# Switching the PE array to the 64-row mode and back once per four chunks instead of once per two, in a kernel that hides convolution work behind its matmuls

**The chip, the cores and the metric.** One core of one Trainium2 chip. The metric is the device time of one execution in microseconds (us), as a median. An execution of one core has no die partner to compare with, so the clock that TensorE was granted is given where it matters: the profiles record it. "PE" is TensorE; its weight loads are a separate stream beside its matmuls.

## The reference

One block of a transformer: a modulated LayerNorm, a long convolution with gates, a residual, a second modulated LayerNorm, and a SwiGLU feed-forward network. S = 2048 rows, D = 576 features, F = 4608 hidden features, all bfloat16. Cut to what matters:

```python
h = layernorm(x) * (1 + ca) + sa
kv = causal_4_tap(k, shift_k) * v
y = irfft(rfft(pad(kv)) * rfft(pad(ssm_k)))[:S] + kv * ssm_D     # the convolution
x = x + ga * (h * y)
h = layernorm(x) * (1 + cb) + sb
x = x + gb * ((silu(h @ w1) * (h @ w3)) @ w2)                    # the feed-forward network
```

The convolution is causal, so rows can be done block by block: the kernel works on four row blocks of 512 rows.

## The kernel before

After an opening, in which the first rows go through the convolution and a half-width first stage of products runs, the kernel has for each of four row blocks a *gate/up stage* (`stream`: `h @ w1` and `h @ w3`, evicted and multiplied) and a *down projection* (`down`: the product with `w2`). The convolution of the next row block is a Python generator of small steps. `advance(cost)` emits steps worth `cost` planned microseconds at that place of the program, so that they run beside the products. Most of the convolution is VectorE work (spectra multiplied and summed), but it also has TensorE matmuls (transposes, spectra at L313, inverse transforms at L539), ScalarE copies of their results, LayerNorm passes on ScalarE, and six tiny scalar computations for each LayerNorm on GpSimd.

A contraction over D = 576 is four full matmuls of 128 rows and 64 rows that are left. The 64-row matmuls of gate and up run two at a time, one in each half of the array, and that needs another row mode of the PE array.

```python
self.psum = pool("psum", bufs=4, ...)   # tiles of two banks: all of PSUM
self.hp = pool("hp", bufs=2)            # staging of sg and u

def full(k, first):     # 8 (or 16 narrow) matmuls over 128 rows, both products
    ...
def rest(k, first):     # the 64-row ones, gate in rows 0-63, up in rows 64-127
    ...
def hide(k):
    (fc, t0, t1, _, _), fi, m = items[k]
    sg = self.hp.tile([P, RB], BF16, name="sg", tag="sg")
    nc.scalar.activation(sg[:], gus[k][:, 0, :], ACT.Silu)              # L934, ScalarE
    u = self.hp.tile([P, RB], BF16, name="u", tag="u")
    nc.scalar.copy(u[:], gus[k][:, 1, :])                               # L936, ScalarE
    f = fc * FC + fi
    nc.vector.tensor_mul(self.h3[:, f:f + m, t0:t1], sg[:]..., u[:]...) # L938, VectorE
    del gus[k]
    self.advance(rate * 2.05)
# begin(k): weights, and gus[k] = a PSUM tile
for k in range(0, len(items), size):
    early, late = range(k, k + size // 2), range(k + size // 2, k + size)
    for m in early:
        begin(m)
        full(m, True)
    for m in early:
        rest(m, False)
    for m in late:
        begin(m)
        rest(m, True)
    for m in early:
        hide(m)
    for m in late:
        full(m, False)
        hide(m)
# ... cut ...
self.stream(r, jobs, rate, 4 if r == NRB - 1 else 2)
```

An item `k` is one PSUM tile of results. A group runs full, half, half, full, so that the mode changes twice per group. The scheduler keeps the order of each engine's instructions as they are emitted, more or less, and in the traces below each engine takes its instructions in that order. Line numbers are those of the kernel that ran: they shift by a line or a few between the kernels (`down` is L979 before and L980 after).

Of the kernel before, what the change touches and what calls it, by code (L numbers as in the profile page):

```python
# [24 lines left out]
NRB = S // RB  # L25
# [18 lines left out]
class _Kernel:  # L44
# [840 lines left out]
    def stream(self, r, jobs, rate, size):  # L885





        nc = self.nc
        hT = self.h2T[r % 2]
        items = []
        for job in jobs:
            m = RB // (job[2] - job[1])
            items += [(job, fi, m) for fi in range(0, FC, m)]
        gus, ws = {}, {}

        def load(job):
            fc, _, _, w, ahead = job  # L900
            if ahead is not None:
                ahead()
            if w is None:
                if fc not in self.w13:
                    self.load_w13(fc)
                w = self.kept[fc] = self.w13.pop(fc)
            ws[job[0:3]] = w


        def full(k, first):  # L910
            (fc, t0, t1, _, _), fi, m = items[k]
            w, n = ws[fc, t0, t1], t1 - t0
            for a in range(m):
                for i in range(2):
                    for ct in range(4):
                        nc.tensor.matmul(gus[k][:, i, a * n:(a + 1) * n],  # L916
                                         w[:, 5 * i + ct, (fi + a) * P:(fi + a + 1) * P], hT[:, ct, t0:t1],
                                         start=(first and ct == 0 and a == 0),
                                         stop=(not first and ct == 3 and a == m - 1))

        def rest(k, first):
            (fc, t0, t1, _, _), fi, m = items[k]
            w, n = ws[fc, t0, t1], t1 - t0
            for a in range(m):
                for i in range(2):
                    rows = slice(64 * i, 64 * i + 64)
                    nc.tensor.matmul(gus[k][:, i, a * n:(a + 1) * n],  # L927
                                     w[rows, 4, (fi + a) * P:(fi + a + 1) * P], hT[rows, 4, t0:t1],
                                     start=(first and a == 0), stop=(not first and a == m - 1))

        def hide(k):
            (fc, t0, t1, _, _), fi, m = items[k]
            sg = self.hp.tile([P, RB], BF16, name="sg", tag="sg")
            nc.scalar.activation(sg[:], gus[k][:, 0, :], ACT.Silu)  # L934
            u = self.hp.tile([P, RB], BF16, name="u", tag="u")
            nc.scalar.copy(u[:], gus[k][:, 1, :])  # L936
            f = fc * FC + fi
            nc.vector.tensor_mul(self.h3[:, f:f + m, t0:t1], sg[:].rearrange("p (a t) -> p a t", a=m),  # L938
                                 u[:].rearrange("p (a t) -> p a t", a=m))
            del gus[k]  # L940
            self.advance(rate * 2.05)

        def begin(k):
            if items[k][1] == 0:
                load(items[k][0])
            gus[k] = self.ps()
# [8 lines that stand above are left out]
                begin(m)  # L955
                rest(m, True)
            for m in early:
                hide(m)
            for m in late:
                full(m, False)  # L960
                hide(m)

    def down(self, r, rate):
        nc = self.nc
# [62 lines left out]
    def row_blocks(self, n1):  # L1027
        for r in range(NRB):
            cost = 0
            if r + 1 < NRB:  # L1030
                s0 = 2 * r + 2

                self.begin(self.conv(s0), FIRST_DUE if r == 0 else 0.0)
                cost = CONV_US[r]
            time = 110.0 * 0.85 - (N1 * 1.03 if r == 0 else 0)
            rate = cost / time
            if r == 0:

                jobs = [(fc, 256, 512, self.kept[fc], None) for fc in (n1 - 2, n1 - 1)]

                new = [(n1 + i, 0, RB, None, (lambda: self.keep_x(0)) if i == 1 else None)
                       for i in range(NF // FC - n1)]
                again = [(fc, 256, 512, None, None) for fc in range(n1 - 2)]
                while new or again:
                    jobs += new[0:1] + again[0:1]
                    new, again = new[1:], again[1:]
            else:
                jobs = [(fc, 0, RB, None, None) for fc in range(NF // FC)]
            self.stream(r, jobs, rate, 4 if r == NRB - 1 else 2)
            self.down(r, rate)  # L1050
            self.end()

# [52 lines left out]
```

## Time and profile before

521.53 us (521.48 to 521.57, three executions); the profiled execution spans 518.3 us.

| stage (from its first matmul to the next stage's) | us |
|---|---|
| opening, to the first transpose of the first row block | 68.9 |
| first block: gate/up, with the transposes ahead of it; down | 62.95; 39.54 |
| second block: gate/up; down | 78.22; 41.31 |
| third block: gate/up; down | 78.29; 38.01 |
| fourth block: gate/up; down (no convolution left) | 71.85; 35.48 |

The chain that ended last, followed back through whatever released each step:

```profile
PE 84%; DMA 8%; ACT 4%; DVE 2%; issue 1%; POOL 1%; DVEq 0%
```

Nearly all of the time is TensorE itself. The second is TensorE's timeline at the start of the first block's convolution. Columns: start, duration, engine, line, operation, output and inputs, count, and in brackets how long the engine was idle just before and what ended that.

```profile
78.81 0.41 PE L313 MATMUL ps<-kT,Fk 128*128 128x288 bf16 x2
79.94 1.91 PE L916 MATMUL ps<-h2T,wst 128*128 128x256 bf16 x16 [0.72 <-ACT W L315]
81.78 0.61 PE L927 MATMUL ps<-h2T,wst 64*128 64x256 bf16 x8
82.78 0.41 PE L313 MATMUL ps<-kv,Fb 128*128 128x288 bf16 x2 [0.39 <-ACT u L936]
```

Between one pair of spectrum matmuls (L313) and the next there is product work, 1.91 + 0.61 us of it here.

### The profile page before, as it was taken

To read this page: it belongs to the slowest core of one execution; us is meant where nothing else is said; L and a number is where in the kernel's file an instruction comes from. 1 tells how busy PE (TensorE), PEld (TensorE's weight loads), DVE (VectorE), ACT (ScalarE), POOL (GpSimd) and SP (SyncE) were. 2 spreads that over 40 slices of the span, in tenths; PEclk is the share of its full clock that TensorE was granted. 3 is DMA by queue.
4 is the path that set the end of the run, shared out by engine and by line. 5 is a ranking of instruction groups with operands and counts; after the bars stand their busy time and mean duration, and the time that the engine had idled before them with its cause. 6 is when DMAs were issued, how large, how long until landed. Compare 5 with 4: busy or idle time off the path is not lost.

```text
span 518.3 us, 8731 instructions
## 1 busy us (share of the span) xinstructions
PE 499.9 (96%) x3362; PEld 293.8 (57%) x3362; DVE 341.0 (66%) x515; ACT 293.3 (57%) x581; POOL 54.9 (11%) x109
## 2 busy tenths in 40 slices
PE   7999988999999999999998999999999999999997
PEld 3666765555788444444676543434588544444775
DVE  8898996999995355896999995389661212222012
ACT  6668469668543469759561465876816446445000
POOL 3205001204021001202002000120101000000000
PEclk9999889999999999999999999999999999999999
DMA  8959629757679953547999894554455453450462
GB/s 269 313 178 332 201 89 321 275 183 250 197 208 348 330 176 107 188 158 275 363 365 352 318 284 150 165 178 156 152 143 145 147 173 119 161 169 10 118 179 70
DMA packets 102205, 107.77 MB, mean 208 GB/s; under 512 B 5075, under 2 KB 94228, under 8 KB 102164
## 3 DMA queue, kind: packets, MB, share of 16 engines
q1 hardware_dynamic: 102142, 107.21, 64.3%
q8 instruction: 26, 0.43, 0.3%
q14 instruction: 15, 0.12, 0.1%
q10 hardware_dynamic: 22, 0.01, 0.0%
HBM read 96.00 MB, written 11.21 MB: 207 GB/s over the span
## 4 chain that ended last, share of the span: by engine, by line
PE 84%; DMA 8%; ACT 4%; DVE 2%; issue 1%; POOL 1%; DVEq 0%
PE ps L916 46%; PE ps L979 25%; PE ps L927 7%; DMA wst<-in_B_w_dram 5%; DMA w2t<-in_B_w_dram 3%; PE ps L313 2%; PE ps L539 2%; PE ps L364 1%; PE ps L299 1%; ACT junk L440 1%; PE ps L571 1%; PE ps L219 0%; PE ps L626 0%; ACT sg L934 0%; DMA shk_raw<-in_A_shift_k_dram 0%
## 5 line engine op out<-in xcount | busy, mean ns | idle before, releaser
L916 PE MATMUL ps<-h2T,wst 128*128 128x512 bf16 (+1 forms) x1344 | 267.4, 351 | 5.9 <-DMA wst<-in_B_w_dram 3.0
L916 PEld LDWEIGHTS <-wst 128*128 128x128 bf16 x1344 | 128.1, 98 | 128.6 <-issue 19.7
L934 ACT ACTIVATE sg<-ps 128x512 bf16<-128x512 f32 x144 | 86.6, 601 | 117.0 <-PE ps L927 73.9
L979 PE MATMUL ps<-w2t,h 128*128 128x288 bf16 x1152 | 145.6, 286 | 3.1 <-DMA w2t<-in_B_w_dram 2.3
L979 PEld LDWEIGHTS <-h 128*128 128x128 bf16 x1152 | 112.2, 98 | 32.5 <-issue 4.0
L938 DVE TENSOR_TENSOR h<-sg,u 128x512 bf16<-128x512 bf16 x144 | 60.5, 422 | 96.6 <-ACT u L936 96.6
L936 ACT CAST u<-ps 128x512 bf16<-128x512 f32 x144 | 84.5, 587 | 0.2 <-DVE h L938 0.2
L410 DVE TENSOR_TENSOR p<-X,V 128x3456 bf16<-128x3456 bf16 x28 | 54.7, 1953 | 5.1 <-DMA X<-Xd 4.9
L412 DVE TENSOR_TENSOR z<-z,p 128x3456 bf16<-128x3456 bf16 x28 | 54.7, 1954 | 0.2
L997 DVE TENSOR_TENSOR og<-ps,gbrow 128x288 bf16<-128x288 f32 x32 | 13.2, 450 | 48.9 <-PE ps L979 48.9
L927 PE MATMUL ps<-h2T,wst 64*128 64x512 bf16 (+1 forms) x336 | 43.2, 355 | 0.4 <-ACT kT L366 0.4
L440 ACT ACTIVATE junk<-x 128x576 bf16<-128x576 bf16 x54 | 37.5, 695 | 0.5
L601 ACT ACTIVATE h2T<-ps,sbcol,cbcol 128x256 bf16<-128x256 bf16 x35 | 16.7, 569 | 24.8 <-PE ps L571 24.8
L927 PEld LDWEIGHTS <-wst 64*128 64x128 bf16 x336 | 11.6, 95 | 28.1 <-issue 24.1
L455 POOL TENSOR_SCALAR l2m<-l2s 128x2 f32<-128x2 f32 x6 | 8.9, 1476 | 153.3 <-ACT junk L440 153.3
L334 DVE TENSOR_TENSOR kvt<-kh,shk 128x1152 bf16<-128x1152 bf16 x24 | 18.1, 753 | 7.4 <-DMA kh<-in_A_k_dram 7.2
L455 POOL TENSOR_SCALAR l1m<-l1s 128x2 f32<-128x2 f32 x7 | 6.5, 929 | 139.4 <-ACT junk L440 139.4
L566 ACT ACTIVATE h2row<-x,l2n,l2r 128x576 bf16<-128x576 bf16 (+1 forms) x24 | 13.7, 642 | 12.5 <-POOL l2n L460 12.4
L335 DVE TENSOR_TENSOR kv<-kv,kvt 128x1152 bf16<-128x1152 bf16 x24 | 18.1, 753 | 0.3
L315 ACT CAST X<-ps 128x576 bf16<-128x576 f32 x24 | 15.5, 658 | 0.0
L405 DVE TENSOR_TENSOR z<-X,V 128x3456 bf16<-128x3456 bf16 x7 | 13.7, 1953 | 2.5 <-DMA X<-Xd 2.5
L745 ACT CAST y<-ps 128x576 bf16<-128x576 f32 x14 | 8.4, 651 | 10.2 <-PE ps L539 10.2
(137 smaller groups left out, 356.3 us busy)
## 6 DMA issues: line engine op xcount, KB each, us to landing
wst<-in_B_w_dram SPq DMA_DIRECT2D x80, 512.0 KB, 4.5
w2t<-in_B_w_dram SPq DMA_DIRECT2D x72, 288.0 KB, 3.2
X<-Xd SPq DMA_DIRECT2D x8, 864.0 KB, 5.8
Xd<-X SPq DMA_DIRECT2D x6, 864.0 KB, 6.4
wst<-in_B_w_dram SPq DMA_DIRECT2D x80, 64.0 KB, 2.2
kh<-in_A_k_dram SPq DMA_DIRECT2D x7, 720.0 KB, 6.9
Vd<-V SPq DMA_DIRECT2D x4, 864.0 KB, 6.3
V<-Vd SPq DMA_DIRECT2D x4, 864.0 KB, 5.0
```

Source lines behind the costliest of these rows:

```text
L334: nc.vector.tensor_mul(tmp[:], kh[:, 3 - j:5 - j, :], tap(j))
L335: nc.vector.tensor_add(kv[:], kv[:], tmp[:])
L410: nc.vector.tensor_mul(p[:], X[:], V[:])
L412: nc.vector.tensor_add(z[:], z[:], p[:])
L440: self.nc.scalar.activation(junk[:], src[:, i, :], func, accum_out=out[:, col:col + 1])
L601: nc.scalar.activation(dst, src, ACT.Identity, bias=self.sbcol[:, ct:ct + 1], scale=self.cbcol[:, ct:ct + 1])
L916: nc.tensor.matmul(gus[k][:, i, a * n:(a + 1) * n], w[:, 5 * i + ct, (fi + a) * P:(fi + a + 1) * P], hT[:, ct, t0:t1], start=(first and ct ...
L927: nc.tensor.matmul(gus[k][:, i, a * n:(a + 1) * n], w[rows, 4, (fi + a) * P:(fi + a + 1) * P], hT[rows, 4, t0:t1], start=(first and a == 0 ...
L934: nc.scalar.activation(sg[:], gus[k][:, 0, :], ACT.Silu)
L936: nc.scalar.copy(u[:], gus[k][:, 1, :])
L938: nc.vector.tensor_mul(self.h3[:, f:f + m, t0:t1], sg[:].rearrange("p (a t) -> p a t", a=m), u[:].rearrange("p (a t) -> p a t", a=m))
L979: nc.tensor.matmul(acc[t], self.h3[:, f0 + f, t * P:(t + 1) * P], w[:, f, :], start=(f0 + f == 0), stop=(f0 + f == NF - 1))
```

## The change

The intent: groups of four in all 512-row stages, so that the mode changes half as often, as the fourth block already did. Because a group of four holds all four PSUM tiles, no convolution step is emitted behind its first two members, and a double portion behind each of the other two, so that a convolution matmul finds a tile that the first members have left. The opening stage keeps its pairs.

```diff
-        def hide(k):
+        def hide(k, go):
@@
-            self.advance(rate * 2.05)
+            if go:
+                self.advance(go * rate * 2.05)
@@
             for m in early:
-                hide(m)
+                hide(m, 1 if size == 2 else 0)
             for m in late:
                 full(m, False)
-                hide(m)
+                hide(m, 1 if size == 2 else 2)
@@
-            self.stream(r, jobs, rate, 4 if r == NRB - 1 else 2)
+            self.stream(r, jobs, rate, 4)
```

## The prediction

> **What bounds the kernel now.** I read the page first, then the chain of waits in two stretches, then busy time by stage, then the VectorE and DMA rows of the one stage where TensorE is not alone.
>
> ```profile
> PE 499.9 (96%) x3362; PEld 293.8 (57%) x3362; DVE 341.0 (66%) x515; ACT 293.3 (57%) x581; POOL 54.9 (11%) x109
> L916 PE MATMUL ps<-h2T,wst 128*128 128x512 bf16 (+1 forms) x1344 | 267.4, 351 | 5.9 <-DMA wst<-in_B_w_dram 3.0
> L927 PE MATMUL ps<-h2T,wst 64*128 64x512 bf16 (+1 forms) x336 | 43.2, 355 | 0.4 <-ACT kT L366 0.4
> ```
>
> TensorE is busy 96% of the span, and the two groups here are the gate/up products: L916 contracts over 128 rows, L927 over the 64 rows left of 576. Mean durations overlap, so I price a matmul by start-to-start distance, from the chain. Second row block (one feature chunk is 16 full matmuls and 4 half-row ones per two chunks), then the last row block, which already has groups of four:
>
> ```profile
> 212.71 0.54 PE ps L927 x4
> 213.25 3.56 PE ps L916 x16
> 216.81 0.54 PE ps L927 x4
> 217.34 3.56 PE ps L916 x16
> ```
>
> ```profile
> 418.86 0.97 PE ps L927 x8
> 419.83 7.01 PE ps L916 x32
> 426.84 0.97 PE ps L927 x8
> ```
>
> Two chunks repeat every 216.81 - 212.71 = 4.10 us, so four cost 8.19 (4.095 x 2 over several periods); a group of four repeats every 426.84 - 418.86 = 7.98. The difference, 0.21 us, is one pair of row-mode changes. It also comes out bottom up: 16 full matmuls with no change before them take 3.45 us (0.2158 each), with a change 3.56; four half-row matmuls run two at a time, 2 x 0.2158 = 0.43, and take 0.54. So each change costs about 0.105 us. Nothing else fills these stretches: the chain is TensorE end to end.
>
> Busy time by stage (first row block's products, second's, last's):
>
> ```profile
> core 0: us, PE busy (x) PEld busy (x) DVE busy (x) ACT busy (x) POOL busy (x), PEclk, DMA share, GB/s
> 72.00:132.60 60.60, 56.98 (x411) 34.48 (x411) 55.48 (x72) 46.22 (x95) 11.06 (x18) 0.97 0.68 228
> 171.60:250.00 78.40, 78.40 (x405) 32.64 (x404) 54.75 (x82) 57.90 (x117) 7.95 (x18) 1.00 0.62 207
> ```
>
> In the second row block TensorE is full and VectorE has slack. In the first, VectorE is busy 55.5 of 60.6 us, and TensorE waits a little, mostly for weights (0.5, 0.5 and 1.1 us at 86, 100 and 127.6).
>
> **What the Trainium skill says.** "TensorEngine Tiling (Array Packing)", Tiling Modes, Key Properties: "Changing tiling mode (not just tile) drains the TensorE". The trace agrees and gives the price, 0.105 us. "TensorE: Matmul & The Clock Gate", Back-to-back issue gap, puts isolated N=512 matmuls at about 216 ns when warm; here 215.8. "PSUM — Partial Sum Buffer", Specifications, gives 8 banks per partition of 512 FP32 values: the pool's four two-bank tiles are all of it, so a group of four holds the whole of PSUM until its first members are evicted. The trace of before cannot show that beside convolution work, since its only groups of four (last row block) have none.
>
> **The change part by part.** *Removed: mode changes.* An item is one fill of a PSUM tile: a chunk of 128 features by 512 rows, or two chunks by 256 rows. The first row block has 24 items after the unchanged opening stage (12 of single chunks, 12 of paired ones), the second and third 36 each. Groups of two make 12 + 18 + 18 = 48 pairs of changes, groups of four 6 + 9 + 9 = 24. Gain 24 x 0.211 = 5.06 us, all on TensorE, all on the path where TensorE is the bound. No matmul is added or dropped.
>
> *Moved: instruction order.* I compared the built orders. In the last group of the second row block the scheduler splits the half-row work: one half-row matmul, eight full, five half-row, two full, two half-row. That is three pairs of changes in place of one, and a half-row matmul alone in its slot: 2 x 0.211 + 0.216 = 0.64 us back.
>
> *Moved: convolution steps.* They now come in two double portions per group. One step unit is 1.037 x 2.05 in the second row block, so 4.25 us of planned work at once, and nothing behind the first two members. In the second and third row blocks I stepped through the groups by hand with before's durations (eviction 2 x 0.5 to 0.6, convolution copy 0.52, product and sum 1.9 each). Relative to the group's start the first two are evicted by about 4.9 and 6.1 us, the third begins full matmuls at 4.5 and ends at 6.3, so a convolution tile issued then finds a free buffer; the fourth ends at 8.0. The inverse transforms (L539) sit after the seventh and eighth group, and VectorE's last input for them is ready at least 0.3 us earlier. I charge no stall but 0.1 here and there: net gain 18 x 0.211 - 0.64 - 0.3 = 2.9 us.
>
> *First row block.* Gain 6 x 0.211 = 1.27, against three losses that I find:
> - First group: the transposes and six spectrum matmuls move behind the third and fourth member. ScalarE then has a chain of four statistics passes (0.68) alternating with four copies (0.52), an eviction and two 0.77 us rows just before the next group, so the next group starts near 85.9 instead of an effective 85.5, and VectorE's first spectrum sum slips from 83.3 to about 86.
> - Weights: two groups mix two weight chunks whose second loads only when the previous group is done (5.5 to 5.7 us in the chain), but its half-row products now come 4.0 us after that and need all four pieces. Before, 4 of its full matmuls could run first. About 0.8 and 0.4 us more wait.
> - The inverse transform there stands between the third and fourth member of the fourth group, and its second half needs a VectorE sum that I place at 111.9, some 1.5 us after TensorE gets there; from then on ScalarE's evictions wait for VectorE's products (two staging buffers only), and the last two groups lose another 1 to 2 us waiting for PSUM.
>
> Together about 4 us lost for 1.27 gained: the first block ends 2.7 us later. The down projection behind it is TensorE-bound and VectorE catches up in it, so the delay stays and does not grow. Sum: 521.5 + 2.7 - 2.9 = 521.3; as my by-hand waits are a pessimistic reading (any slack that I missed shortens them), I put 520.9.
>
> **The rivals.**
> 1. *Pure saving*: TensorE stays the only bound, the waits in the first block don't appear. For it: second and third block show no TensorE wait at all, and VectorE's order is nearly unchanged in item numbers. Against: VectorE is busy 92% in the first block and starts later. Time 521.5 - 5.06 + 0.64 = 517.1.
> 2. *PSUM starvation*: with all four tiles held, convolution tiles wait for evictions in every group, about 1 us in each of the 12 groups of the second and third block that have convolution matmuls. For it: four buffers, double portions. Against: the built order puts these matmuls where before's durations find free tiles. Time 521.3 + 12 = 533 at worst, 525 with a third of it.
> 3. *Weight loads become the bound*: 8.0 instead of 8.2 us per weight chunk; loads land in 4.5 us median and the last block runs at 7.98 with no weight wait, so only the mixed groups of the first block are exposed, as counted.
>
> **Range and chances.** Between rival 1 and a mild form of rival 2: 517.0 to 525.0 holds it 8 times in 10. Two per cent is 10.4 us. Faster by that would need double the whole of the removed cost; slower needs rival 2 in full. Hence 0.01 faster, 0.96 within, 0.03 slower.
>
> **What would show each step.** Right: in the second and third block the chain repeats every 7.98 us with 7.01 and 0.97 us pieces wherever there is no convolution matmul; one stretch near the end of the second block with a lone half-row matmul; TensorE's waits on weights in the first block growing to about 1.4 us each, a wait of L539 on VectorE there, and TensorE idle of 4 us or so more than now in that stage, whose end moves from 132 to about 135. Wrong: waits of L313 or L916 on ScalarE spread over all groups (rival 2), or a first block that ends at 131 or earlier (rival 1). A period other than 7.98 would void the price of a change itself.

## The result

**529.55 us** (527.43 to 530.08, four executions) against 521.55 us (521.48 to 522.79) on the same chip: ratio 1.014, 95% interval 1.0108 to 1.0172. A ratio here is the mean time of one kernel's fast executions over that of the other's in the same rounds, so it is not quite the ratio of the medians. Executions over 1.5% slower than the fastest of the same kernel are left out of the means. The changed kernel is 8 us slower, inside the 2% class and outside the predicted range of 517 to 525 us. The clock is not the reason: its executions were granted 0.990 to 0.997 of full speed, and its profiled execution took 527.43 us at 0.997 where that of the kernel before took 520.12 us at 0.992.

The profiled executions span 525.5 and 518.3 us. The stages, from the two traces:

| stage | before | after | difference |
|---|---|---|---|
| opening (unchanged code) | 68.94 | 67.63 | -1.31 |
| first block gate/up | 62.95 | 66.79 | +3.84 |
| first block down | 39.54 | 40.33 | +0.79 |
| second block gate/up | 78.22 | 79.84 | +1.62 |
| second block down | 41.31 | 41.56 | +0.25 |
| third block gate/up | 78.29 | 79.41 | +1.12 |
| third block down | 38.01 | 38.89 | +0.88 |
| fourth block, both | 107.33 | 107.32 | 0 |

They sum to +7.2 us, which is the difference of the spans. The page's lines that answer to those of before, and its chain:

```profile
PE 496.5 (94%) x3362; PEld 296.6 (56%) x3362; DVE 341.6 (65%) x515; ACT 292.2 (56%) x581; POOL 47.2 (9%) x109
...
PE 64%; DVE 16%; ACT 10%; DMA 7%; issue 3%; POOL 1%; SPq 0%; ACTq 0%
...
L916 PE MATMUL ps<-h2T,wst 128*128 128x512 bf16 (+1 forms) x1344 | 263.0, 349 | 6.5 <-DMA wst<-in_B_w_dram 1.8
...
L927 PE MATMUL ps<-h2T,wst 64*128 64x512 bf16 (+1 forms) x336 | 39.3, 348 | 1.1 <-ACT u L936 0.8
```

TensorE is busy for 3.4 us less (499.9 to 496.5), so part of the saving is there, but not all of the 3.4 us is saving: 1.5 us of it lies in the first block, where the clock differed. Before's profile has a stretch at half clock there, which that of the changed kernel has not (first block of each; then that stretch):

```profile
68.94:131.89 62.95, 58.09 (x424) 35.17 (x422) 57.76 (x76) 48.37 (x99) 11.06 (x18) 0.97 0.66 219
67.63:134.42 66.79, 56.59 (x425) 35.43 (x422) 57.31 (x76) 47.97 (x99) 9.66 (x18) 1.00 0.68 212
73.02:76.43 3.41, 3.41 (x27) 2.22 (x25) 3.34 (x3) 1.14 (x3) 0.00 (x0) 0.50 0.00 0
```

The columns are those of the prediction (start and end, length, busy us of PE, PEld, DVE, ACT and POOL, then granted clock, DMA share and GB/s). The same code at a clock of 1.00, in run 4's profile below, takes 61.97 us in the first block. So at like clocks the first block loses 4.8 us, and not 3.84. The other gate/up stages ran at 1.00 in every profile of this document, so their lengths compare directly; the first block's clock lies between 0.95 and 1.00.

The span grew, and the chain says who took over: TensorE's share fell from 84% to 64%, and VectorE's rose from 2% to 16% and ScalarE's from 4% to 10%. The saving itself is in the second block just as predicted:

```profile
221.76 0.97 PE ps L927 x8
222.73 7.01 PE ps L916 x32
229.74 0.97 PE ps L927 x8
```

Busy time of the second block's stage, with the same columns:

```profile
174.75:254.59 79.84, 77.57 (x405) 33.86 (x403) 53.70 (x82) 56.38 (x114) 5.90 (x18) 1.00 0.62 203
```

In the second block TensorE, which had no idle time at all before, is now idle for 79.84 - 77.57 = 2.27 us, in four waits: 0.74 and 0.27 us for a convolution copy (X, L315), and these two for an eviction copy:

```profile
235.92 0.41 PE L313 MATMUL ps<-kv,Fb 128*128 128x288 bf16 x2 [0.68 <-ACT u L936]
236.90 3.61 PE L916 MATMUL ps<-h2T,wst 128*128 128x512 bf16 x16 [0.57 <-ACT u L936]
```

The eviction of that group begins at 234.80 us, 0.1 us after a product of VectorE's (L938) that stood behind a step of 1.96 us. Three places in the other blocks show the same kinds of wait.

**First block, first group.** The same spectrum matmuls as above, now all behind the third and fourth member:

```profile
80.38 0.71 ACT L440 ACTIVATE junk<-x 128x576 bf16<-128x576 bf16 x1
...
81.06 0.65 ACT L315 CAST W<-ps 128x576 bf16<-128x576 f32 x1
...
81.76 0.41 PE L313 MATMUL ps<-kv,Fb 128*128 128x288 bf16 x2 [0.80 <-ACT W L315]
...
82.96 0.41 PE L313 MATMUL ps<-kv,Fb 128*128 128x288 bf16 x2 [0.80 <-ACT Wo L315]
...
84.16 1.02 PE L916 MATMUL ps<-h2T,wst 128*128 128x512 bf16 x4 [0.80 <-ACT Wo L315]
```

No product matmuls stand between the last of them any more. The three shown wait for the copy of an earlier spectrum, which gives back a PSUM tile; ScalarE makes these copies at its own pace of one LayerNorm pass and one copy, 1.2 us per 0.41 us of TensorE work. With a wait of 0.77 us at 79.36 us, for the copy of the transposed rows (kT, L366), that makes four waits, which replace the 0.72 and 0.39 us of before.

**First block, inverse transform.** TensorE stands still for VectorE's sums:

```profile
106.95 0.76 DVE L525 TENSOR_TENSOR z<-z 128x1152 bf16<-128x1152 bf16 x1
107.62 1.96 DVE L410 TENSOR_TENSOR p<-X,V 128x3456 bf16<-128x3456 bf16 x1
...
109.49 0.76 DVE L526 TENSOR_TENSOR z<-z 128x1152 bf16<-128x1152 bf16 x1
...
110.31 0.66 PE L539 MATMUL ps<-z,Fb 128*128 128x288 bf16 x4 [1.87 <-DVE z L526]
```

A step of 1.96 us from another part of the convolution stands between the two sums in VectorE's queue.

**Third block, first group.** This is the longest single wait of the two full stages, and it goes through three engines:

```profile
302.11 1.96 DVE L410 TENSOR_TENSOR p<-X,V 128x3456 bf16<-128x3456 bf16 x1
...
303.99 0.75 DVE L938 TENSOR_TENSOR h<-sg,u 128x512 bf16<-128x512 bf16 x2
304.50 0.60 ACT L934 ACTIVATE sg<-ps 128x512 bf16<-128x512 f32 x1 [2.31 <-DVE h L938]
...
304.99 0.58 ACT L936 CAST u<-ps 128x512 bf16<-128x512 f32 x1
305.46 1.14 ACT L366 COPY kT<-ps 128x1152 bf16<-128x1152 bf16 x1
...
306.65 0.65 PE L313 MATMUL ps<-kT,Fk 128*128 128x288 bf16 x4 [1.79 <-ACT kT L366]
```

VectorE is in a long step, so two products (L938) wait. The two staging buffers are full, so ScalarE's next eviction waits 2.31 us. The convolution's copy stands behind that eviction in ScalarE's queue, and TensorE waits 1.79 us for the copy. ScalarE's waits of this kind in the whole kernel (us in total, times, longest), before and after:

```profile
ACT sg L934 <- DVE h L938: 7.4, 6, 1.7
```

```profile
ACT sg L934 <- DVE h L938: 11.9, 10, 2.3
```

### The profile page after: what moved, and what is told of

The parts are those of the page before. It is cut to its first block, busy times and chain, and to the rows that moved or that the text cites. A ratio compares the mean times of both kernels' runs of the same rounds, so it can differ in the third digit from the quotient of the medians.

```text
span 525.5 us, 8723 instructions
## 1 busy us (share of the span) xinstructions
PE 496.5 (94%) x3362; PEld 296.6 (56%) x3362; DVE 341.6 (65%) x515; ACT 292.2 (56%) x581; POOL 47.2 (9%) x109
## 4 chain that ended last, share of the span: by engine, by line
PE 64%; DVE 16%; ACT 10%; DMA 7%; issue 3%; POOL 1%; SPq 0%; ACTq 0%
PE ps L916 35%; PE ps L980 17%; PE ps L927 5%; DVE p L410 5%; DVE z L412 3%; ACT junk L440 3%; DMA h<-in_w_mod_dram 2%; ACT sg L934 2%; ACT u L936 2%; DMA wst<-in_B_w_dram 2%; PE ps L539 1%; ACT hg L500 1%; DVE h L938 1%; DMA w2t<-in_B_w_dram 1%; DMA V<-Vd 1%
## 5 line engine op out<-in xcount | busy, mean ns | idle before, releaser
L916 PE MATMUL ps<-h2T,wst 128*128 128x512 bf16 (+1 forms) x1344 | 263.0, 349 | 6.5 <-DMA wst<-in_B_w_dram 1.8
L938 DVE TENSOR_TENSOR h<-sg,u 128x512 bf16<-128x512 bf16 x144 | 59.9, 423 | 103.3 <-ACT u L936 103.2
L927 PE MATMUL ps<-h2T,wst 64*128 64x512 bf16 (+1 forms) x336 | 39.3, 348 | 1.1 <-ACT u L936 0.8
L927 PEld LDWEIGHTS <-wst 64*128 64x128 bf16 x336 | 13.6, 94 | 25.1 <-issue 17.1
L455 POOL TENSOR_SCALAR l2m<-l2s 128x2 f32<-128x2 f32 x6 | 3.3, 556 | 155.2 <-ACT junk L440 155.2
L539 PE MATMUL ps<-z,Fb 128*128 128x288 bf16 x80 | 11.8, 287 | 4.9 <-DVE z L526 3.4
L455 POOL TENSOR_SCALAR l1m<-l1s 128x2 f32<-128x2 f32 x7 | 2.7, 382 | 152.4 <-ACT junk L440 152.4
L315 ACT CAST X<-ps 128x576 bf16<-128x576 f32 x24 | 15.3, 657 | 0.0
```

The lines of the kernel that those rows point to most:

```text
L539: nc.tensor.matmul(ps[:, h, 0:H], self.Fb[:, b, cs], z[:, row, h * H:(h + 1) * H], start=(i == 0), stop=(i == len(terms) - 1))
L916: nc.tensor.matmul(gus[k][:, i, a * n:(a + 1) * n], w[:, 5 * i + ct, (fi + a) * P:(fi + a + 1) * P], hT[:, ct, t0:t1], start=(first and ct ...
L927: nc.tensor.matmul(gus[k][:, i, a * n:(a + 1) * n], w[rows, 4, (fi + a) * P:(fi + a + 1) * P], hT[rows, 4, t0:t1], start=(first and a == 0 ...
L938: nc.vector.tensor_mul(self.h3[:, f:f + m, t0:t1], sg[:].rearrange("p (a t) -> p a t", a=m), u[:].rearrange("p (a t) -> p a t", a=m))
```

## The experiments

Four theories grew in this order. **A**: holding all four PSUM tiles turns any delay of an eviction into a stall. **B**: portions that are held back and doubled bunch the convolution and make VectorE late. **C**, from the second run: VectorE's unbroken runs starve GpSimd, and ScalarE stands behind GpSimd. **D**, after eleven runs: the two staging buffers carry VectorE's delay over to ScalarE and from there to TensorE. "First block" below is always counted from its transposes. All eighteen gave right results. "Before" is the kernel before, timed in the same rounds; its medians were 521.4 to 522.1 us. A stage length is from one profiled execution.

**1 and 2: each half of the change alone.** Groups of four with one portion behind every member:

```diff
-                hide(m, 1 if size == 2 else 0)   # early
+                hide(m, 1)
-                hide(m, 1 if size == 2 else 2)   # late
+                hide(m, 1)
```

> Groups of four in every full stage, but convolution steps behind every member in single portions, as before. Theory A (the loss comes from holding all four PSUM tiles while convolution work needs tiles too): as slow as the changed kernel or slower, 528 to 533 us, because convolution matmuls now stand right behind the half-row matmuls, when no tile is free until the first member is evicted. Rival B (the loss comes from doubling and delaying the convolution portions): near the pure saving, 516 to 519 us.

Measured: 528.85 us, ratio 1.0106 (1.0067 to 1.0146). The second block's stage takes 81.36 us, longer than in the changed kernel. This is theory A, in one line of the waits (us in total, times, longest):

```profile
PE ps L313 <- ACT u L936: 5.7, 10, 0.9
```

Ten times a spectrum matmul needs a PSUM tile, and every one is held by a member of the group that ScalarE is still evicting. The down projections of the first and third block stay at 39.74 and 38.12 us. That of the second has 45.26 us, with a wait of ScalarE for GpSimd of 12.7 us in it. The total is in theory A's range.

Pairs as before, but no portion behind the first and a double one behind the second member:

```diff
-                hide(m, 1 if size == 2 else 0)   # early, the three blocks
+                hide(m, 0)
-                hide(m, 1 if size == 2 else 2)   # late
+                hide(m, 2)
-            self.stream(r, jobs, rate, 4)
+            self.stream(r, jobs, rate, 4 if r == NRB - 1 else 2)
```

> Groups of two as before in the first three row blocks, but no steps behind the first member and a double portion behind the second. Theory A: two tiles stay free, so little is lost, 521 to 523.5 us. Rival B: loses what the changed kernel loses plus the saving that it does not have, 528 to 535 us.

Measured: 533.41 us, ratio 1.0222 (1.018 to 1.0264): slower than the whole change, with two PSUM tiles free. So neither half is innocent, and the halves do not add. The first block takes 70.39 us (at a clock of 0.96), and the largest part of that excess is one event:

```profile
122.31 9.30 POOL L455 TENSOR_SCALAR l2m<-l2s 128x2 f32<-128x2 f32 x1 [25.61 <-ACT junk L440]
...
133.42 2.29 ACT L566 ACTIVATE h2row<-x,l2n,l2r 128x576 bf16<-128x576 bf16 x4 [8.60 <-POOL l2n L460]
...
136.71 1.22 PE L364 MATMUL ps<-ident,knat 128*128 128x128 bf16 x10 [5.73 <-ACT u L936]
```

A GpSimd instruction on two numbers per partition lasts 9.30 us where its neighbours last 0.2 to 0.7. It ends at 131.61 us, 0.09 us after VectorE's run of back-to-back two-input instructions. ScalarE waits for it, the evictions behind that in its queue wait, PSUM stays full, and TensorE stands for 5.73 us.

**3 and 4: where, and the price.** The changed kernel with the first block back in pairs, and the kernel before with its fourth block in pairs too:

```diff
-            self.stream(r, jobs, rate, 4)
+            self.stream(r, jobs, rate, 4 if r else 2)      # run 3
-            self.stream(r, jobs, rate, 4 if r == NRB - 1 else 2)
+            self.stream(r, jobs, rate, 2)                  # run 4
```

> The changed kernel with groups of two and single portions in the first row block alone. If the losses of the blocks add up as its trace shows (3.8 us in the first block's products, 0.8 in the down projection behind it, 1.6 and 1.1 in the second and third block's products): 529.5 - 4.6 = about 525 us. If the later losses were only an echo of a late first block: 517 to 519 us.

> The kernel before with groups of two in the last row block, which has no convolution work beside it: nine more pairs of row-mode changes at 0.211 us. If the price read from the chain holds: 521.5 + 1.9 = 523.4 us. If a change is hidden or dearer in some other way: outside 522.9 to 523.9.

Measured: 522.64 us, ratio 1.0007 (0.9974 to 1.004), which is between the two expectations, and 523.3 us, ratio 1.002 (0.9996 to 1.0043). With the first block in pairs, that block takes 62.43 us and its down projection 39.46 us, as before. The second and third stage still take 79.85 and 79.56 us. The two kinds of reading do not quite agree here. By the stages from the transposes on, run 3 loses 4.4 us against the profile of before, about half of the changed kernel's 8.5. By the medians it loses 0.5 us. Its executions had higher clocks (mean of the four 0.996, of the eleven of before 0.992), and its interval reaches to +0.4%, 2 us. What is safe is that the first block is a large part of the loss and not all of it. In the fourth run the fourth stage goes from 71.85 to 73.74 us: +1.89 us for nine more pairs of changes, 0.210 us a pair. The price in the prediction holds, and where there is no convolution work it is paid out in full.

**5, 6 and 7: theory C.** One VectorE copy of GpSimd's result just ahead of ScalarE's use of it. VectorE has to stop there until GpSimd has been served.

```diff
                 yield -waits[2]
+                nc.vector.tensor_copy(self.small.tile([P, 2], F32, name="seen", tag="seen")[:], b[:])
                 with self.behind(nc.scalar):
                     self.normed_act(s, r, b)
```

On the kernel of run 2, on the changed kernel, and on the kernel before:

> The second experiment (pairs, portions none/double in the first three blocks; 533.41 us) with one VectorE copy of the two values that GpSimd ends the second LayerNorm with, placed just ahead of ScalarE's use of them: VectorE has to stop until GpSimd has been served. Theory C (GpSimd is starved by VectorE's unbroken runs, and ScalarE's evictions stand behind it): the 9.3 us instruction of GpSimd is gone, ScalarE's waits for it fall from 17.7 us to under 9, the stall of 5.7 us near 131 us is gone, total 526 to 529 us. Theory B alone (the VectorE work itself is late, GpSimd only reports it): nothing gained, as the added copy makes VectorE later still, 533 to 535 us.

> The changed kernel with the same VectorE copy. Theory C as the main cause of the loss: total falls from 529.6 to 523 us or less. Theory A (four PSUM tiles held) or B (VectorE late with its portions) as the main cause: only the 2 us wait of ScalarE near 130 us is shortened, total 528 to 530 us.

> Control: the kernel before with the same VectorE copy. All theories: within 0.7 us of the kernel before, six copies of some 0.1 us on an engine that has room; if it is more, what the two runs above show must be corrected by it.

Measured: 528.0 us, ratio 1.0114 (1.0081 to 1.0146), so 5.4 us better than run 2 (of other rounds); 533.38 us, ratio 1.0222 (1.0179 to 1.0264), outside both expectations; and 521.57 us, ratio 0.9982 (0.9954 to 1.0009). In run 5 VectorE stops at 128.33 us for 1.89 us, GpSimd's stuck instruction ends 0.08 us after that stop, and TensorE's wait of 5.73 us is 1.40. The instruction is shorter and not gone (4.90 us), and ScalarE's waits for GpSimd fall from 17.7 to 10.8 us, not under 9. Theory C is right for run 2 in kind. As the cause of the changed kernel's loss it falls: run 6 did not gain. It lost against the changed kernel, partly at a lower clock (0.983 to 0.997), and its profile shows longer waits of L539 for VectorE's sums (1.87 us in the second down projection, 2.10 in the third), as one would expect where VectorE is stopped on purpose.

**8: groups of three.** One member full first, two after it:

```diff
-                hide(m, 1 if size == 2 else 2)
+                hide(m, {2: 1, 3: 1.5, 4: 2}[size])
-            self.stream(r, jobs, rate, 4)
+            self.stream(r, jobs, rate, 4 if r == NRB - 1 else 3)
```

> Groups of three in the first three blocks (one member whole rows first, two after; no steps behind the first, one and a half portions behind each of the other two; the fourth block keeps four). 16 of the 24 pairs of mode changes are saved, 3.4 us, and a group holds three of the four PSUM tiles. Theory A (holding all four tiles turns each delay of an eviction into a stall): gate/up stages of the second and third block 76.9 to 77.3 us (before 78.2), total 517.5 to 520 us. Theory B (portions held back and bunched keep VectorE late): half to two thirds of the loss stays, these stages 78 to 79 us, down projections still 0.5 us longer, total 521 to 526 us.

Measured: 528.41 us (523.46 to 530.85), ratio 1.0107 (1.0065 to 1.015). The profiled execution is the fastest of the six, so its stages are the best case: second and third stage 77.59 and 78.52 us, together 0.4 us less than before, but 67.89 us in the first block. The second block comes near theory A's 76.9 to 77.3 us, the third does not, and the total belongs to neither: 16 saved pairs do not help a first block that loses 4.9 us, whose longest wait is 2.63 us of L313 for VectorE.

**9: the last group in pairs.** The changed kernel, with the last four items of each of the first three stages as two pairs:

```diff
-        for k in range(0, len(items), size):
+        size4 = size == 4 and r + 1 < NRB
+        cuts = [(k, size) for k in range(0, len(items) - (size if size4 else 0), size)]
+        if size4:
+            cuts += [(len(items) - 4, 2), (len(items) - 2, 2)]
+        for k, size in cuts:
```

> The changed kernel with only the last four items of the first three gate/up stages put back into two pairs with one portion behind each member: three more pairs of mode changes, 0.63 us. Theory B (in the changed kernel VectorE enters each down projection with up to a whole double portion undone, and the convolution's inverse matmul waits for its sums): the waits of that matmul in the three down projections (0.4, 1.1 and 0.9 us) shrink to under 0.4 us each, the down projections take 39.5, 41.3 and 38.0 us within 0.5 us, total 528 us or less. Rival (VectorE is late by more than one portion from the whole stage, so that the last group does not matter): waits unchanged, total 530 us.

Measured: 530.02 us, ratio 1.015 (1.0115 to 1.0185). L539's waits in the three down projections (0.40, 1.10 and 0.93 us) are now under 0.15, 0.36 and under 0.15 us. So that delay does come from the double portions of the last group. But the time did not follow: TensorE now waits 1.49 and 1.03 us for evictions at the start of the second and third down projection. The wait moved by one place; the three down projections take 39.93, 43.11 and 38.56 us. The expectation is half met, and the total is the rival's.

**10: pairs, threes, threes, fours, with the copy of run 5.**

```diff
-            self.stream(r, jobs, rate, 4 if r == NRB - 1 else 3)   # run 8
+            self.stream(r, jobs, rate, (2, 3, 3, 4)[r])
```

> First block in pairs as before, second and third block in groups of three, fourth in fours, with the VectorE copy that lets GpSimd in. Pairs of mode changes saved: 12, 2.53 us. Theory A (a group of four leaves the convolution no PSUM tile, a group of three leaves one; the first block does not bear grouping): gate/up stages of the second and third block 77.0 to 78.3 us, first block as before, total 519 to 522 us, a gain of up to 2.5 us. Rival (it is holding the portions back that costs, in threes as in fours): stages 78.3 us or more and down projections 0.5 us longer, total 522 to 525 us.

Measured: 524.59 us, ratio 1.0062 (1.0029 to 1.0095). The total is in the rival's range. The second stage takes 77.72 us, as A has it; the third takes 81.51 us, mostly because its first group waits 2.89 us for VectorE to empty the accumulators of the down projection before it. The late VectorE finds another way to TensorE.

**11: one PSUM tile less, no portion moved.** The kernel before with:

```diff
-        self.psum = pool("psum", bufs=4, ...)
+        self.psum = pool("psum", bufs=3, ...)
-            tail = r == NRB - 1 and h == 1       # four separate accumulators
+            tail = False
-            self.stream(r, jobs, rate, 4 if r == NRB - 1 else 2)
+            self.stream(r, jobs, rate, 2)
```

> The kernel before with three PSUM tiles of two banks in place of four; pairs everywhere, the fourth block too (+1.9 us as measured), and the last down projection without its four separate accumulators. No portion is moved and no mode change saved. It leaves the convolution one free tile beside a pair, as a group of three does with four. Theory A: the first three gate/up stages get longer by 1 to 4 us each, with waits of the convolution's matmuls for ScalarE's eviction copies of 0.3 to 1 us each, as the experiment with groups of four and equal portions shows them. Rival (free tiles do not matter, the portions do): these stages within 0.5 us of before, total 523 to 524.5 us.

Measured: 541.38 us, ratio 1.0366 (1.0334 to 1.0398). The first three stages are 4.9, 3.3 and 5.7 us longer. Free PSUM tiles matter more than A had guessed, with no portion moved and no mode change saved. The waits are spread over convolution copies, eviction copies and the down projection's accumulators. (The fourth block's pairs and the lost separate accumulators are in the total, but not in these three stages.)

**12 to 15: theory D.** ScalarE's first pass writes silu straight into the place of the product, so that VectorE multiplies in place, and `u` gets four buffers in about the same memory.

```diff
-            sg = self.hp.tile([P, RB], BF16, name="sg", tag="sg")
-            nc.scalar.activation(sg[:], gus[k][:, 0, :], ACT.Silu)
+            f = fc * FC + fi
+            sg = self.h3[:, f:f + m, t0:t1]
+            nc.scalar.activation(sg, gus[k][:, 0, :].rearrange("p (a t) -> p a t", a=m), ACT.Silu)
@@
-        self.hp = pool("hp", bufs=2)
+        self.hp = pool("hp", bufs=4)
```

On the kernel before, on the changed kernel, and on those of runs 1 and 8:

> Control: the kernel before, with the first eviction pass written straight into the place of the product and four staging buffers for the second. All theories: within 1.5 us of before; ScalarE's waits for VectorE's products (7.4 us in the trace of before) go to under 2 us, but TensorE hardly waits on them there.

> The changed kernel with the same deep staging. If staging is the link (VectorE late, two buffers, ScalarE held, PSUM held): ScalarE's waits for products fall from 11.9 us to under 3, TensorE's 1.8 us wait at 304.9 us goes, the first block gets 1 to 2 us shorter, third block's stage 78.3 us or less, total 523 to 526 us. If the link is PSUM itself (theory A) or VectorE's sums for the inverse: 528 to 531 us.

> Groups of four with equal portions (528.85 us) and deep staging. Theory A (the convolution's tile waits for an eviction copy, which VectorE has no part in): the waits of 0.5 us of its matmuls for the copy stay, second block's stage still 80.5 to 81.5 us, total 527 to 530 us. If staging is the link here too: stage under 79.5 us, total 525 us or less.

> Groups of three (528.41 us) and deep staging. If one free PSUM tile is enough and staging was what held it back: 519 to 522 us, first block within 1.5 us of before. Otherwise 526 to 529 us.

| run | us | ratio (95%) | second stage | third stage | first block |
|---|---|---|---|---|---|
| 12, before + deep | 521.95 | 1.0014 (0.9975 to 1.0053) | 78.22 | 78.31 | 62.03 |
| 13, changed + deep | 526.78 | 1.0123 (1.0083 to 1.0164) | 78.38 | 77.11 | 67.66 |
| 14, run 1 + deep | 523.19 | 1.0067 (1.0021 to 1.0112) | 80.37 | 79.28 | 64.31 |
| 15, run 8 + deep | 526.77 | 1.0119 (1.0079 to 1.016) | 77.53 | 78.11 | 66.79 |

Run 14's median is that of its five fast executions; a sixth, 531.98 us, counts as slow. The first block's clock was 1.00, 0.95, 1.00 and 1.00 in these four profiles. In run 12 ScalarE no longer waits for products at all, and nothing is gained, as expected.

The same place of the third block in run 13 as shown above of the changed kernel:

```profile
302.10 1.96 DVE L410 TENSOR_TENSOR p<-X,V 128x3456 bf16<-128x3456 bf16 x1
...
303.58 0.60 ACT L935 ACTIVATE h<-ps 128x512 bf16<-128x512 f32 x1 [0.40 <-PE ps L916]
...
304.54 1.14 ACT L366 COPY kT<-ps 128x1152 bf16<-128x1152 bf16 x1
...
305.73 0.53 PE L313 MATMUL ps<-kT,Fk 128*128 128x288 bf16 x3
```

VectorE is in the same long step, yet ScalarE's eviction no longer waits for it (0.40 us, and that for TensorE), the copy comes in time, and L313 has no wait. None of ScalarE's evictions in run 13 waits for a product any more. The third stage falls from 79.41 to 77.11 us, 1.2 us under the kernel before, and the second from 79.84 to 78.38: its two waits for eviction copies are gone, and those for convolution copies, 0.74 and 0.27 us, stay. So D is the link in these two stages. (The edit changes two things, the number of buffers and the place that silu is written to; they were not separated.) The down projections do not gain: 39.42, 42.38 and 38.91 us. In the first block the lengths (66.79 and 67.66 us) cannot be compared, as run 13 has two stretches at half clock there and the changed kernel has none:

```profile
111.58:114.99 3.41, 3.20 (x15) 2.20 (x16) 3.41 (x6) 0.64 (x1) 0.00 (x0) 0.50 0.01 4
132.06:135.47 3.41, 3.41 (x18) 2.45 (x17) 2.48 (x2) 2.71 (x6) 0.66 (x1) 0.50 0.59 189
```

TensorE's waits of over 0.15 us in that block say more. They fall from 9.97 to 8.00 us: the last groups' waits for ScalarE go from 3.37 to 0.84 us (to 1.80 in run 18 below, which has the same last groups at the full clock), and the inverse transform's wait stays (2.36 and 2.47 us). So staging seems to carry a part of the first block's loss too, which the lengths cannot show. In the totals the gain (529.55 to 526.78 us, of different rounds) lies inside the overlap of the two intervals; the stages show it, not the totals, and the total is over the 523 to 526 us expected. (Run 13 had the lower clocks, 0.984 to 0.993 against 0.990 to 0.997.)

In run 14 the waits for the eviction copy stay at 0.54 to 0.91 us each and the second stage at 80.37 us, hardly under A's range: that part of A has nothing to do with staging. Its total is below A's range mostly because the second down projection took 39.97 us in place of run 1's 45.26, with ScalarE's longest wait for GpSimd at 5.6 us. In run 15 the first block again has a wait of L313 for VectorE (3.17 us), and the total is that of the second expectation.

**16 to 18: what is left.** Deep staging with the blocks as pairs, fours, fours, fours; as pairs, threes, fours, fours; and the kernel of run 13 with only the first four items of the first block back in two pairs:

```diff
-            self.stream(r, jobs, rate, 4)
+            self.stream(r, jobs, rate, 4 if r else 2)        # run 16
+            self.stream(r, jobs, rate, (2, 3, 4, 4)[r])      # run 17, portions as in run 8
+        cuts = [(k, size) for k in range(0, len(items), size)]   # run 18
+        if r == 0 and size == 4:
+            cuts = [(0, 2), (2, 2)] + cuts[1:]
```

> Deep staging, first block in pairs, the other three in fours with none/none/double/double portions. If the stages add as measured apart (first block and its down projection as in the kernel before, second and third gate/up stage 78.4 and 77.1 us, their down projections 0.5 to 1 us longer): total 520 to 522 us, no more than 1 us from before. Rival (a loss of the fours that moves rather than adds): over 523 us.

> Deep staging, blocks in pairs, threes, fours, fours. If the stages add: 77.5 and 77.1 us for the second and third stage, total 519.5 to 521.5 us, the best of all by a little. Rival as above: over 523 us.

> The changed kernel with deep staging (526.78 us), only the first four items of the first block put back into two pairs (one pair of mode changes more, 0.2 us). If the first group's run of waits is local: three of the waits of 0.8 us near 82 us go, first block 1.5 to 2.5 us shorter (65 to 66 us from the transposes on), the wait of the inverse matmul for VectorE (2.5 us) stays, total 524.5 to 526 us. If VectorE's lateness there comes from the first group too: the wait of the inverse matmul falls under 1 us as well, first block 63.5 to 64.5 us, total 523 to 524.5 us.

Measured: 522.05 us, ratio 0.9994 (0.9947 to 1.0042); 520.45 us, ratio 0.9983 (0.9954 to 1.0012); 525.59 us, ratio 1.0092 (1.006 to 1.0124). Both totals come out as expected within 0.1 us, and stages do add: run 16 has 78.38 and 77.12 us, and run 17 has 77.36 and 77.11. Together with 0.9 us more in the third down projection (38.91) and a first block of 63.6 to 63.8 us in these two profiles (at a clock of 0.97, as in the profile of before with 62.95), what is won disappears in the spread. Run 17 is the fastest of all by median, but its interval holds 1, so it does not beat the kernel before. In run 18 the row of 0.8 us waits is gone (0.72 and 0.39 us again, as before), while L539 still waits 1.89 us for VectorE's sum. So that row is the first group's own, and VectorE's lateness 25 us later does not come from it. What is won by removing it stays open: the first block is 1.57 us shorter than in run 13, but has one stretch at half clock where run 13 has two, each of which can cost up to half of 3.41 us (an estimate from the stretches shown above). TensorE's waits in the block sum to 8.15 us, against 8.00 in run 13, whose last groups ran at half clock: waits for weights (1.56 us against 0.86) and three of 0.19 us at the start of the block stand in place of the row.

## Why the prediction was wrong

What held, by its own steps:

- *The price of a mode change* and *the 24 pairs saved*. Run 4 gives 0.210 us a pair against 0.211, and the 7.98 us period appears in the second block. *The split half-row work* at the end of the second block is in the trace at 247 to 252 us, in three pieces as read from the built order.
- *The end of the first block*: 134.4 us against "about 135". That is luck: the opening, unchanged code, was 1.31 us shorter in this profile, and the block's loss was predicted as 2.7 us and measured as 3.84, or 4.8 at like clocks. The prediction's own losses, as it lists them, sum to 4.1 to 5.1 us, of which it took the least. The sizes were off too, and cancelled in part. TensorE's waits of over 0.15 us in this block went from 4.86 to 9.97 us in sum, +5.11, and less the 1.27 us saved that is the +3.84 measured. That this closes is chance, since it leaves out the clock: against run 4's profile of the same code, with 4.89 us of waits, about 1 us of the 4.8 stays unaccounted for. The *first group* costs +2.06 us (predicted about 0.4): the copies and LayerNorm passes were counted in ScalarE's chain, but not that each spectrum matmul in a row exposes one of them. The *inverse transform's wait* is +2.36 us (predicted 1.5). The *last groups* cost +3.37 us (predicted 1 to 2), of which some lie behind ScalarE's wait of 2.04 us for GpSimd near 130 us, which the prediction did not consider. The *weight waits* were the miss in the other direction: predicted +1.2, measured -2.12 us. All three weight waits of before are gone, probably because a stage that is held up elsewhere gives the loads time. The remaining -0.56 us are waits at the start that are not there after.

What failed:

1. *"I charge no stall but 0.1 here and there: net gain 18 x 0.211 - 0.64 - 0.3 = 2.9 us"* for the second and third block. Measured: a loss of 1.62 + 1.12 = 2.7 us, so this one term is off by 5.6 us, most of the miss of 529.55 - 520.9 = 8.65 us. (The 0.4 us that the prediction took off at the end, because its waits were "a pessimistic reading", went the wrong way as well.) The reading by hand followed TensorE and ScalarE with each eviction starting when its matmuls were done. It left out that an eviction also needs a staging buffer, which VectorE gives back, and that the doubled portions put VectorE's 1.96 us steps in front of the products. The two-buffer limit stood in the prediction, but only for the first block. Run 13 shows the link: with it cut, the two stages together gain 1.0 us instead of losing 2.7. The other 1.9 us of the predicted gain are not accounted for one by one; run 13 still has waits such as 0.74 us for a convolution copy.

2. *"VectorE catches up in it, so the delay stays and does not grow"* for the down projections. They grew by 0.79, 0.25 and 0.88 us in the changed kernel. Run 9 shows that the double portions of the last group are what VectorE is late with: L539's waits shrank with them, though not the time. For the third block's down projection this is firm: 38.01 to 38.02 us in the profiles of before, of run 4 and of run 12, and 38.89 to 38.91 in those of the changed kernel and of runs 3, 13, 16, 17 and 18. (Run 7, the kernel before with a VectorE copy, has 38.87, with a wait of L539 too.) For the first and second it cannot be told: the same code took 39.54 and 41.31 us in the profile of before, and 40.02 and 42.41 in that of run 4.

3. *Rival 2, PSUM starvation*, was given little weight because "the built order puts these matmuls where before's durations find free tiles". In the changed kernel that was half right. Its sign came, but not in all groups: two waits for eviction copies in the second block (0.68 and 0.57 us) and two in the third (0.17 and 0.35). Holding back the portions does its job, since with equal portions the second stage is worse (81.36 against 79.84 us), with the waits that rival 2 names. But a free tile on paper is one whose eviction is on time, and run 11 shows how narrow that is.

Still open: of the first block's loss, the first group's row of waits is shown to be its own (run 18), but not what it costs in the end, and the inverse transform's wait is seen in every profile that combines fours and held-back portions there. What makes VectorE late by 2 us there, rather than by less as with either half alone (the block takes 63.96 us with equal portions and 64.30 in run 5, both at a clock of 1.00), was not separated further. Over 61.97 us, the same code as before at that clock, these are 2.0 and 2.3 us (the second with run 5's copy in it); in this block the two halves nearly add up to the 4.8 us of the whole change.

The prediction also sets its 215.8 ns beside a figure for isolated matmuls; it was measured in a back-to-back stream of matmuls with their weight loads.

## What to carry to other kernels

Before making groups larger to save a fixed cost on the bounding engine, list everything that a member holds until it is done, PSUM tiles and staging buffers alike, and ask of each which engine gives it back and what stands before that in its queue. Filler work that is spread thin also covers its own latencies; bunched, as in the first group here, each of its steps exposed one. Here the fixed cost was won back in full only in the stage where nothing else shares the buffers, 1.89 us in the fourth block, which already had it. And compare stage lengths only after comparing the granted clock of these very stages: a mean over the whole execution hides a stretch at half clock.

## What the Trainium skill lacked or had wrong

- "TensorEngine Tiling (Array Packing)", Tiling Modes, Key Properties, says that a change of tiling mode drains TensorE but gives no price. Here eighteen changes more cost 1.89 us (71.85 to 73.74 us), 0.105 us each.
- "SBUF — State Buffer", Who interferes with whom, says that a VectorE instruction with two SBUF inputs contends with a GpSimd instruction that reads SBUF, and of 2-port modes that whoever is first gets the port pair "for the whole instruction". The trace agrees that there is blocking, but it lasted far longer than one instruction: one GpSimd instruction on 128x2 values was held for 9.30 us, across a dozen back-to-back VectorE instructions of at most 1.94 us, and ended 0.09 us after the last of them. In run 5 it ended 0.08 us after VectorE stopped. The page does not say that a run without gaps can starve GpSimd throughout; that the port is the means is the page's statement and was not tested here.
- I found on no page how far the granted clock moves single-core times: in these runs the kernel before took 516.93 us at a mean clock of 1.000 and, on another chip, 525.39 us at 0.987. The mean clock is not all of it: at 0.993 its nineteen executions lie between 518.57 and 522.62 us. One stretch of 3.41 us at half clock went with 1.0 us in the first block (62.95 us, against 61.97 for the same code without it).
